# Two chunks of the next unit's first weights split earlier at the end of a pair of token slots

## The chip, the cores and the metric

One Trainium2 chip, one NeuronCore of it. The metric is device time in microseconds for one execution of the program, as the median of several runs. The core has five engines that run side by side, each its own instruction stream in program order: PE (TensorE, matrix products; PEld is its weight load), DVE (VectorE), ACT (ScalarE), POOL (GpSimd) and SP (SyncE, which only issues transfers).

## What is computed

Three layers in a row, all in 32-bit floating point: attention with random features, a feed-forward layer with softplus, and a layer of 8 experts of which each token uses one. The change lies in the last:

```python
# x: 2304 tokens x 512; E = 8 experts; w1: 8 x 512 x 1024; w2: 8 x 1024 x 512
logits = xn @ en.T / tau
expert_idx = np.argmax(logits, axis=1)
...
for e in range(E):
    mask = expert_idx == e
    h = np.maximum(x[mask] @ w1[e], 0.0)
    out[mask] = gate_w[mask, None] * (h @ w2[e])
```

## The kernel before

Tokens are sorted to experts on the chip. They are packed into slots of 128 tokens that share an expert. A unit is one slot (a single) or two slots of the same expert (a pair): first four singles, then six times a pair and a single in turn, then one more single. Two further pairs stand behind conditions at the end and run only if the routing needs them. The last 260 us of the span are these alternating units.

Each unit needs its expert's weights: `w1r` (4 chunks of 128 rows x 1024) and `w2r` (8 chunks of 128 x 512), which POOL fetches by an indirect transfer two units ahead (`fetch_w`), into one of two buffers each. PE does not multiply 32-bit numbers exactly in one pass, so every operand is split into a high and a low half: ACT casts to the high half (line 1246), DVE subtracts it from the source to get the low half (line 1250), and each product is made of three passes, high by high, high by low and low by high (`PASSES`, line 1269). The split of a chunk of first weights is `unit_w1(g, c)`, of a chunk of second weights `unit_w2(g, c)`, of the transposed token rows `unit_x(g)`. The split tiles of first weights have one buffer for each chunk and half (`wi0` to `wi7`, line 1310). So chunk c of the next unit can be split only when the present unit has used its own chunk c for the last time.

A pair works in four quarters of the hidden layer. `pair_m1(g, k)` (line 1358) makes a hidden quarter of both slots, 24 matmuls of 256 columns, six for each chunk of first weights in turn. `split(*hidden(k), ...)` takes it through relu into halves: ACT at line 1241 (`mh_h`), DVE at line 1242 (`mh_l`). `pair_m2(g, k)` (line 1382) multiplies it with two chunks of second weights into the two slots' outputs `po`, 12 matmuls of 512 columns. A single does two hidden halves: `slot_m1` (line 1335, 12 matmuls of 512 columns; for the first half in the order high and low rows by the high half of chunks 0 to 3, then high rows by the low halves, line 1275), `slot_relu` (ACT, `hs`), `slot_t` (PE transposes `pt_h`, then a split), and `slot_m2`. `unit_out` scales `po` on ACT into `ot` and has POOL scatter it to the output.

From the second unit on nothing is reordered (`tc.manual_schedule`, line 1545): each engine runs its instructions in the order in which `unit(g)` writes them (line 1395). In it `w1_(c)` splits chunk c of the next unit's first weights, `w2_(c)` of its second weights. At the end of a pair the order is: products of the last hidden quarter, three chunks of second weights, split of that hidden quarter, second products of the third quarter, the next unit's token rows, all four chunks of its first weights, second products of the last quarter, outputs, two more chunks of second weights. The next unit then starts with `slot_m1(g, 0)`.

Of the kernel before, what the change touches and what calls it, by code (L numbers as in the profile page):

```python
# [76 lines left out]
def tile_kernel(ctx, tc, q, k, v, omega, w_in, w_out, emb, tau, w1, w2, out):  # L77
# [1138 lines left out]
    def fetch_w(s, which="12", chain=0):  # L1216
        for nm, src in (("w1r", w1v), ("w2r", w2v)):
            if nm[1] not in which:
                continue
            if s < 2:  # L1220
                raw_w[nm, s] = mraw.tile([P, NC * F2], F32, name=f"{nm}{s}")
            with tc.issue_after(marks["x"]) if chain and "x" in marks and s < 4 else ExitStack():
                nc.gpsimd.indirect_dma_start(
                    out=raw_w[nm, s % 2], out_offset=None, in_=src,
                    in_offset=bass.IndirectOffsetOnAxis(ap=w_idx[:, s:s + 1].bitcast(U32), axis=0),
                    bounds_check=E * P - 1, oob_is_err=False)

    def fetch_x(g):
        t = xpool.tile([P, 2, YW], F32, tag="xhi", name="xg")
        for i, s in enumerate(groups[g]):  # L1230
            nc.gpsimd.indirect_dma_start(
                out=t[:, i, :], out_offset=None, in_=(ya if s < NS_A else yb)[:, :],
                in_offset=bass.IndirectOffsetOnAxis(ap=g_idx[:, s:s + 1].bitcast(U32), axis=0),
                bounds_check=NT - 1, oob_is_err=False)
            xgs[s] = t[:, i, :]
            if s >= NS_A:
                marks["x"] = traced()

    def split(hi, lo, lo_eng, src, relu=False, hi_eng="a"):
        if relu:  # L1240
            nc.scalar.activation(out=hi, in_=src, func=AF.Relu)
            nc.vector.scalar_tensor_tensor(out=lo, in0=src, scalar=0.0, in1=hi.bitcast(F32),
                                           op0=ALU.max, op1=ALU.subtract)
        else:
            if hi_eng == "a":
                nc.scalar.copy(out=hi, in_=src)  # L1246
            else:
                (nc.gpsimd if hi_eng == "p" else nc.vector).tensor_copy(hi, src)
            eng = nc.gpsimd if lo_eng == "p" else nc.vector
            eng.tensor_tensor(out=lo, in0=src, in1=hi.bitcast(F32), op=ALU.subtract)  # L1250
# [55 lines left out]
    def unit_w1(g, c):  # L1306
        if (g, c) in w1s:
            return
        r = raw_w["w1r", g % 2][:, c * F2:(c + 1) * F2]
        t = [wpool.tile([P, F2], F32R, tag=f"wi{2 * c + i}", name=f"w1_{c}_{i}") for i in range(2)]  # L1310
        if len(groups[g]) == 1:
            o, r = [x.rearrange("q (h p c) -> q h p c", h=2, c=4) for x in t], \
                r.rearrange("q (p h c) -> q h p c", h=2, c=4)
        else:

            o, r = [x.rearrange("q (k p j) -> q k p j", k=4, j=2) for x in t], \
                r.rearrange("q (p k j) -> q k p j", k=4, j=2)
        kind = 0 if g < 2 else len(groups[g])
        split(*o, TUNE["w1"][kind][c], r, hi_eng=TUNE["w1h"][kind][c])
        w1s[g, c] = t  # L1320

    def unit_w2(g, c):
        if (g, c) in w2s:
            return
        r = raw_w["w2r", g % 2][:, c * DM:(c + 1) * DM]
        w2s[g, c] = [wpool.tile([P, DM], F32R, tag=f"wo{2 * c + i}", name=f"w2_{c}_{i}") for i in range(2)]
        split(*w2s[g, c], TUNE["w2"][g >= 2][c], r, hi_eng=TUNE["w2h"][g >= 2][c])
# [3 lines left out]
    def hidden(key):  # L1331
        hs[key] = [ring.tile([P, 512], F32R, tag=f"wo{x}", name=f"mh_{x}") for x in "hl"]
        return hs[key]

    def slot_m1(g, half, part=slice(0, 12)):
        if part.start == 0:
            hs["ps", half] = mpsum("h", "ph")
        ph = hs["ps", half]
        w = slice(half * HF, half * HF + HF)
        mms = [(xs[g][a][c], w1s[g, c][b_][:, w]) for c, (a, b_) in first_order(half)]  # L1340
        for i in range(part.start, part.stop):
            x, r = mms[i]
            nc.tensor.matmul(ph, lhsT=x, rhs=r, start=(i == 0), stop=(i == 3 * NC - 1))  # L1343

    def slot_relu(half):
        hs["row"] = mraw.tile([P, HF], F32, tag="hs", name="hs")
        nc.scalar.activation(out=hs["row"], in_=hs["ps", half], func=AF.Relu)
# [10 lines left out]
    def pair_m1(g, k):  # L1358

        ph = hs["ps"] = mpsum("h", "ph")  # L1360
        order = first_order(k)
        for n, (c, (a, b_)) in enumerate(order):
            for j in range(2):
                f = slice(2 * k * P + j, 2 * (k + 1) * P, 2)
                nc.tensor.matmul(ph[:, j * 256:j * 256 + 256], lhsT=w1s[g, c][b_][:, f],  # L1365
                                 rhs=xs[g][a][c].rearrange("p i t -> p (i t)"),
                                 start=(n == 0 and j == 0), stop=(n == len(order) - 1), skip_group_check=True)

    def unit_m2(g, i, parts):

        s = groups[g][i]
        if parts[0][2] == 0:
            po[s] = mpsum("o", "po")
        for h, o, c in parts:
            for n, (a, b_) in enumerate(PASSES):
                nc.tensor.matmul(po[s], lhsT=h[a][:, o:o + P], rhs=w2s[g, c][b_], start=(c == 0 and n == 0),  # L1376
                                 stop=(c == 7 and n == 2))
# [4 lines left out]
    def pair_m2(g, k):  # L1382
        for i in range(2):
            unit_m2(g, i, [(hs[k], 256 * j + P * i, 2 * k + j) for j in range(2)])

    def unit_out(g):
        for s in groups[g]:
            xt = xgs.pop(s)
            ot = xpool.tile([P, DM], F32, tag="xlo", name="ot")
            nc.scalar.activation(out=ot, in_=po.pop(s), func=AF.Copy, scale=xt[:, DM:YW])  # L1390
            nc.gpsimd.indirect_dma_start(  # L1391
                out=out, out_offset=bass.IndirectOffsetOnAxis(ap=s_idx[:, s:s + 1].bitcast(U32), axis=0),
                in_=ot, in_offset=None, bounds_check=NT - 1, oob_is_err=False)

    def unit(g):
        nxt = g + 1 < NG_ALL
        ahead = g + 2 < NG_ALL

        def w1_(*cs):
            for c in cs:  # L1400
                if nxt:
                    unit_w1(g + 1, c)

        def w2_(*cs):
            for c in cs:
                if nxt:
                    unit_w2(g + 1, c)

        def fetch():
            if ahead:  # L1410
                fetch_x(g + 2)
                fetch_w(g + 2, "2", 1)

        def own(*cs):
            for c in cs:
                unit_w2(g, c)

        if ahead:
            fetch_w(g + 2, "1", 1)
        if len(groups[g]) == 2:  # L1420
            pair_m1(g, 0)
            own(2, 3, 4)
            split(*hidden(0), "v", hs["ps"], relu=True)
            pair_m1(g, 1)
            own(5)
            split(*hidden(1), "v", hs["ps"], relu=True)
            pair_m2(g, 0)
            pair_m1(g, 2)
            own(6, 7)
            fetch()  # L1430
            w2_(0)
            split(*hidden(2), "v", hs["ps"], relu=True)
            pair_m2(g, 1)
            pair_m1(g, 3)
            w2_(1, 2, 3)
            split(*hidden(3), "v", hs["ps"], relu=True)
            pair_m2(g, 2)
            if nxt:
                unit_x(g + 1)
            w1_(0, 1, 2, 3)  # L1440
            pair_m2(g, 3)
            unit_out(g)
            w2_(4, 5)
        else:
            if g > 0:
                slot_m1(g, 0)
            own(2, 3, 4)
            slot_relu(0)
            slot_m1(g, 1, slice(0, 5))
            own(5)  # L1450
            slot_t(0)
            slot_m1(g, 1, slice(5, 12))
            own(6, 7)
            slot_relu(1)
            slot_m2(g, 0, (0, 1))
            w1_(0)
            slot_t(1)
            slot_m2(g, 0, (2, 3))
            if nxt:
                unit_x(g + 1)  # L1460
            w1_(1, 2, 3)
            slot_m2(g, 1, (0, 1))
            if g == 2:
                tokens(bm_b, NT_T, NS_A, NS_B, mpsum("o", "Lb"))
            fetch()
            slot_m2(g, 1, (2, 3))
            unit_out(g)
            w2_(0, 1)
# [74 lines left out]
    for g in range(TUNE["man"]):  # L1543
        unit(g)
# [51 lines left out]
```

## Time and profile before

| what | us |
|---|---|
| median of three runs | 940.6 |
| the three runs | 940.16, 940.6, 946.91 |
| the profiled execution, its own time | 942.76 |
| its span, from the first to the last instruction | 940.9 |

The profile is of one execution. Its page gives the busy time of each engine, the views after it (waits, stretches, timelines) the single instructions with their start in us from the span's start. A timeline row merges neighbours of one kind: start, length of the whole piece, engine, line, operation, written tile and read tiles, count; brackets give the engine's idle time ahead of it and what ended that. The length of a piece of matmuls ends with the last one's modelled end, which is later than the start of the next. In the trace both kinds of weights' split tiles are called `w`; which are meant is told by the source, `w1r` or `w2r`, or by the line of the product.

### The profile page before, as it was taken

The page shows a single profiled execution, that of the slowest core. Times are in us where ns is not written, and L with a number is a line of the kernel's source. Part 1 is how long each engine was busy: PE and PEld are TensorE (multiplying, and loading weights), DVE is VectorE, ACT ScalarE, POOL GpSimd, SP SyncE. Part 2 cuts the span into 40 slices and gives each one's busy share as a digit, 9 for nine tenths or more (in the row PEclk, how much of TensorE's full clock was granted, in tenths as well). Part 3 has the DMA queues.
Part 4 walks back from the last instruction along what each step waited for, and adds up shares of the span by engine and source line. Part 5 has one row for each costly group of instructions (what it writes and reads, how often), then busy time and mean ns, then how long its engine had stood idle before and what let it go on. Part 6 is the DMA issues. An engine that isn't in the chain of part 4 may idle for free. (4 is left out here: it accounts for less than half of the span.)

```text
span 940.9 us, 14526 instructions
## 1 busy us (share of the span) xinstructions
PE 891.9 (95%) x4951; PEld 744.5 (79%) x4951; DVE 689.8 (73%) x1376; ACT 652.8 (69%) x1452; POOL 323.0 (34%) x341
## 2 busy tenths in 40 slices
PE   6898899999999999998999999999999999999993
PEld 6775555588898889987888889888797888988972
DVE  6769888477888887679886777767977676685772
ACT  4897344477878877775877687876867576585672
POOL 1224102155545754575653020012243242241310
PEclk9899999999999999999999999999999999999998
DMA  6625663011362231011301381102023660551910
GB/s 165 166 76 152 185 217 113 17 35 37 57 146 72 45 93 35 20 35 23 68 7 23 81 344 46 34 12 57 26 65 142 276 243 30 211 209 41 356 58 6
DMA packets 86540, 94.69 MB, mean 101 GB/s; under 512 B 50294, under 2 KB 74870, under 8 KB 84160
## 3 DMA queue, kind: packets, MB, share of 16 engines
q1 hardware_dynamic: 77888, 45.21, 18.5%
q0 software_dynamic: 8576, 48.52, 13.7%
q8 instruction: 41, 0.67, 0.3%
q14 instruction: 35, 0.29, 0.1%
HBM read 108.36 MB, written 15.48 MB: 132 GB/s over the span
## 5 line engine op out<-in xcount | busy, mean ns | idle before, releaser
L1376 PE MATMUL po<-w,mh_h 128*128 128x512 f32 x368 | 118.0, 402 | 0.5 <-ACT mh_h L1354 0.5
L1250 DVE TENSOR_TENSOR w<-w2r,w 128x512 fp32r<-128x512 f32 x136 | 88.4, 684 | 17.5 <-ACT w L1246 17.5
L703 PE MATMUL y<-woh,gh 128*128 128x512 f32 x240 | 96.2, 408 | 1.7 <-DVE gh L682 1.7
L1246 ACT CAST w<-w2r 128x512 fp32r<-128x512 f32 x136 | 78.7, 628 | 23.3 <-DMA w2r<-in_moe_w_dram,w_idx 12.8
L703 PE MATMUL y<-wol,gh 128*128 128x512 f32 x240 | 93.9, 395 | 0.0
L1391 POOL DMA_INDIRECT out_dram<-ot,s_idx x23 | 31.5, 1369 | 171.0 <-ACT ot L1390 126.5
L1250 DVE TENSOR_TENSOR w<-w1r,w 128x1024 fp32r<-128x1024 f32 x68 | 80.4, 1226 | 11.1 <-ACT w L1246 11.0
L703 PE MATMUL y<-woh,gl 128*128 128x512 f32 x240 | 81.7, 404 | 0.0
L598 DVE TENSOR_TENSOR wil<-win,wih 128x512 fp32r<-128x512 f32 x72 | 58.4, 811 | 29.1 <-ACT wih L597 28.9
L1376 PEld LDWEIGHTS po<-w,mh_h 128*128 128x128 f32 x368 | 66.9, 191 | 12.2 <-ACT mh_h L1354 0.7
L638 PE MATMUL h<-xhi,wih 128*128 128x384 f32 x320 | 73.0, 348 | 3.2 <-DVE t L657 2.9
L1246 ACT CAST w<-w1r 128x1024 fp32r<-128x1024 f32 x68 | 72.0, 1119 | 3.5 <-PE ph L1343 2.1
L1376 PE MATMUL po<-w,mh_l 128*128 128x512 f32 x184 | 73.4, 399 | 0.9 <-DVE mh_l L1356 0.9
L610 POOL TENSOR_TENSOR wol<-wout,woh 128x512 fp32r<-128x512 f32 x40 | 55.0, 1376 | 45.3 <-ACT woh L609 45.2
L638 PE MATMUL h<-xlo,wih 128*128 128x384 f32 x320 | 70.2, 337 | 0.0
L638 PE MATMUL h<-xhi,wil 128*128 128x384 f32 x320 | 69.9, 339 | 0.0
L1365 PE MATMUL ph<-mxh,w 128*128 128x256 f32 x384 | 62.6, 285 | 0.4
L638 PEld LDWEIGHTS h<-xhi,wih 128*128 128x128 f32 x320 | 55.4, 188 | 8.3 <-DVE t L657 3.7
L425 POOL TENSOR_TENSOR xf<-xf,rc 128x256 f32<-128x256 f32 (+1 forms) x20 | 17.3, 867 | 122.0 <-ACT rc L424 114.8
L638 PEld LDWEIGHTS h<-xhi,wil 128*128 128x128 f32 x320 | 57.7, 188 | 0.3
L1365 PEld LDWEIGHTS ph<-mxh,w 128*128 128x128 f32 x384 | 55.0, 195 | 2.9 <-ACT w L1246 1.6
L638 PEld LDWEIGHTS h<-xlo,wih 128*128 128x128 f32 x320 | 56.4, 188 | 0.0
(311 smaller groups left out, 2376.6 us busy)
## 6 DMA issues: line engine op xcount, KB each, us to landing
wst<-in_moe_w_in_dram SPq DMA_DIRECT2D x16, 512.0 KB, 4.5
wst<-in_moe_w_out_dram SPq DMA_DIRECT2D x16, 512.0 KB, 4.3
raw<-in_k_dram SPq DMA_DIRECT2D x32, 128.0 KB, 2.4
vf<-in_v_dram SPq DMA_DIRECT2D x64, 64.0 KB, 2.3
raw<-in_q_dram SPq DMA_DIRECT2D x32, 128.0 KB, 2.6
ya<-yt SPq DMA_DIRECT2D x20, 128.2 KB, 4.4
yb<-yt SPq DMA_DIRECT2D x20, 128.2 KB, 4.0
ya<-yt SPq DMA_DIRECT2D x8, 256.5 KB, 5.7
```

The source lines that it names most:

```text
L425: nc.gpsimd.tensor_tensor(out=xf, in0=xf, in1=rc, op=ALU.mult)
L598: feng("il", n).tensor_tensor(out=il, in0=wi, in1=ih.bitcast(F32), op=ALU.subtract)
L610: feng("ol", n).tensor_tensor(out=ol, in0=wo, in1=oh.bitcast(F32), op=ALU.subtract)
L638: nc.tensor.matmul(h[:, 0:G], lhsT=a[:, c, :], rhs=x[:, c, :], start=(i == 0), stop=(i == last))
L703: nc.tensor.matmul(y, lhsT=x[:, c], rhs=w, start=(f == 0 and i == 0), stop=(f == NF - 1 and i == len(passes) - 1))
L1246: nc.scalar.copy(out=hi, in_=src)
L1250: eng.tensor_tensor(out=lo, in0=src, in1=hi.bitcast(F32), op=ALU.subtract)
L1365: nc.tensor.matmul(ph[:, j * 256:j * 256 + 256], lhsT=w1s[g, c][b_][:, f], rhs=xs[g][a][c].rearrange("p i t -> p (i t)"), start=(n == 0 an ...
L1376: nc.tensor.matmul(po[s], lhsT=h[a][:, o:o + P], rhs=w2s[g, c][b_], start=(c == 0 and n == 0), stop=(c == 7 and n == 2))
L1391: nc.gpsimd.indirect_dma_start(out=out, out_offset=bass.IndirectOffsetOnAxis(ap=s_idx[:, s:s + 1].bitcast(U32), axis=0), in_=ot, in_offset ...
```

## The change

The splits of chunks 0 and 1 of the next unit's first weights are written earlier in the pair's part of `unit(g)`: chunk 0 ahead of the split of the last hidden quarter, chunk 1 behind that split and ahead of the next token rows. Chunks 2 and 3 stay where all four were. It applies to the six pairs that have a next unit.

```diff
             pair_m2(g, 1)
             pair_m1(g, 3)
             w2_(1, 2, 3)
+            w1_(0)
             split(*hidden(3), "v", hs["ps"], relu=True)
             pair_m2(g, 2)
+            w1_(1)
             if nxt:
                 unit_x(g + 1)
-            w1_(0, 1, 2, 3)
+            w1_(2, 3)
             pair_m2(g, 3)
             unit_out(g)
```

On ACT, at the end of the first pair; `w_c_0` read from `w1r` is the high half of chunk c, `mh_h` that of the last hidden quarter, `mx` that of the next token rows:

```order
 L1246 CAST w_3_0_8620<-w2r_6603 128x512
-L1241 ACTIVATE mh_h<-ph 128x512
+L1246 CAST w_0_0_8624<-w1r_6599 128x1024
+L1241 ACTIVATE mh_h<-ph 128x512
+L1246 CAST w_1_0_8644<-w1r_6599 128x1024
 L1246 CAST mx<-pt_x 128x512
-L1246 CAST w_0_0_8648<-w1r_6599 128x1024
-L1246 CAST w_1_0_8652<-w1r_6599 128x1024
 L1246 CAST w_2_0_8656<-w1r_6599 128x1024
 L1246 CAST w_3_0_8660<-w1r_6599 128x1024
```

The cast of chunk 0 has moved ahead of the relu, that of chunk 1 between the relu and the token rows; two casts are left behind the rows.

On DVE, at the same place; `w_c_1` is the low half of chunk c, `mh_l` that of the hidden quarter:

```order
 L1250 TENSOR_TENSOR w_3_1_8621<-w2r_6603,w_3_0_8620 128x512
-L1242 SCALAR_TENSOR_TENSOR mh_l<-ph,mh_h 128x512
+L1250 TENSOR_TENSOR w_0_1_8625<-w1r_6599,w_0_0_8624 128x1024
+L1242 SCALAR_TENSOR_TENSOR mh_l<-ph,mh_h 128x512
+L1250 TENSOR_TENSOR w_1_1_8645<-w1r_6599,w_1_0_8644 128x1024
 L1250 TENSOR_TENSOR mx<-pt_x,mx 128x512
-L1250 TENSOR_TENSOR w_0_1_8649<-w1r_6599,w_0_0_8648 128x1024
-L1250 TENSOR_TENSOR w_1_1_8653<-w1r_6599,w_1_0_8652 128x1024
 L1250 TENSOR_TENSOR w_2_1_8657<-w1r_6599,w_2_0_8656 128x1024
 L1250 TENSOR_TENSOR w_3_1_8661<-w1r_6599,w_3_0_8660 128x1024
```

The subtractions have moved in the same way. The order of PE, POOL and SP is the same as before.

## Rows read from the trace of the kernel before

**Rows 1.** The page, busy time of each engine over the span.

```profile
PE 891.9 (95%) x4951; PEld 744.5 (79%) x4951; DVE 689.8 (73%) x1376; ACT 652.8 (69%) x1452; POOL 323.0 (34%) x341
```

**Rows 2.** Waits from 700 us on: us in total, times, the longest.

```profile
ACT w L1246 <- DMA w2r<-in_moe_w_dram,w_idx: 12.8, 5, 3.3
...
PE ph L1343 <- DVE w L1250: 2.3, 6, 0.4
...
PE ph L1343 <- ACT w L1246: 1.3, 6, 0.2
```

**Rows 3.** Stretches, first, last of six: us; busy PE, PEld, DVE, ACT, POOL; clock, DMA.

```profile
711.69:718.96 7.27, 6.67 (x29) 4.76 (x28) 5.57 (x9) 6.02 (x11) 2.04 (x2) 1.00 0.10 36
...
899.91:907.18 7.27, 6.66 (x29) 4.76 (x28) 5.58 (x9) 6.02 (x11) 1.86 (x1) 1.00 0.11 38
```

**Rows 4.** Timeline of PE around the second boundary, from pair to single.

```profile
740.94 0.41 PE L1365 MATMUL ph<-mxl,w 128*128 128x256 f32 x2
...
743.34 0.63 PE L1376 MATMUL po<-w,mh_h 128*128 128x512 f32 x2
...
746.09 0.63 PE L1265 MATMUL pt_x<-ident,xg 128*128 128x128 f32 x4
746.48 0.72 PE L1376 MATMUL po<-w,mh_h 128*128 128x512 f32 x2
747.04 0.40 PE L1376 MATMUL po<-w,mh_l 128*128 128x512 f32 x1
...
749.34 1.65 PE L1343 MATMUL ph<-w,mx 128*128 128x512 f32 x6
751.20 1.43 PE L1343 MATMUL ph<-w,mx 128*128 128x512 f32 x5 [0.21 <-ACT w L1246]
753.02 1.65 PE L1343 MATMUL ph<-w,mx 128*128 128x512 f32 x6 [0.39 <-DVE w L1250]
754.50 0.63 PE L1265 MATMUL pt_h<-ident,hs 128*128 128x128 f32 x4
```

**Rows 5.** Timeline of PE, first products of the last single, behind a single.

```profile
913.67 4.21 PE L1343 MATMUL ph<-w,mx 128*128 128x512 f32 x17
```

**Rows 6.** Timeline of ACT around the second boundary.

```profile
743.54 0.60 ACT L1241 ACTIVATE mh_h<-ph 128x512 fp32r<-128x512 f32 x1 [2.25 <-PE ph L1365]
746.76 0.59 ACT L1246 CAST mx<-pt_x 128x512 fp32r<-128x512 f32 x1 [2.62 <-PE pt_x L1265]
747.25 3.90 ACT L1246 CAST w<-w1r 128x1024 fp32r<-128x1024 f32 x4
751.05 1.26 ACT L1390 ACTIVATE ot<-po,xg 128x512 f32<-128x512 f32 x2
752.20 1.13 ACT L1246 CAST w<-w2r 128x512 fp32r<-128x512 f32 x2
753.55 0.60 ACT L1347 ACTIVATE hs<-ph 128x512 f32<-128x512 f32 x1 [0.22 <-PE ph L1343]
```

**Rows 7.** Timeline of DVE around the second boundary.

```profile
744.17 0.69 DVE L1242 SCALAR_TENSOR_TENSOR mh_l<-ph,mh_h 128x512 fp32r<-128x512 f32 x1 [2.16 <-ACT mh_h L1241]
747.38 0.69 DVE L1250 TENSOR_TENSOR mx<-pt_x,mx 128x512 fp32r<-128x512 f32 x1 [2.52 <-ACT mx L1246]
748.33 4.63 DVE L1250 TENSOR_TENSOR w<-w1r,w 128x1024 fp32r<-128x1024 f32 x4 [0.25 <-ACT w L1246]
```

**Rows 8.** Timeline of POOL: the fetch of first weights used at the second boundary.

```profile
720.08 1.04 POOL L1223 DMA_INDIRECT w1r<-in_moe_w_dram,w_idx  x1 [0.30 <-issue]
```

**Rows 9.** All of w1r: duration ns min/median/max, first and last start; transfer to landing.

```profile
L1246 ACT CAST w<-w1r x68: 1031/1052/1344, 552.7 to 913.5; 128x1024 fp32r<-128x1024 f32 x68
L1250 DVE TENSOR_TENSOR w<-w1r,w x68: 1201/1222/1278, 559.4 to 914.9; 128x1024 fp32r<-128x1024 f32 x68
...
DMA to landing us min/median/max: 2.1/8.3/11.5
```

## The prediction

> **What bounds the kernel now.** I read the page's first part, then the table of waits of the last third, then the stretches around the place of the change, then the timelines of PE, ACT and DVE there. PE is busy for 95% of the span and no other engine passes 79% [rows 1], so time can only be won where PE stands still or starts late. In the table of waits, 700 us to the end, PE's first products (line 1343) wait six times for ACT's `w` and six times for DVE's `w` [rows 2]. Six is the number of pairs that run, each followed by a single slot. The stretch from such a single's first product to its first second product takes 7.27 us at the first and at the last of the six boundaries, at a granted clock of 1.00 (the 2.4 GHz level), with PE busy 6.67 us [rows 3]. So the stall is the same at each, and one boundary can stand for all.
>
> At the second boundary PE reads: last quarter of the pair from 746.48, the single's first products at 749.34, a restart at 751.20 behind ACT, another at 753.02 behind DVE, the transposes of the hidden row at 754.50 [rows 4]. The busy share hides part of the loss, since a matmul's modelled end outlasts the next start; I count from start to start. The pace without such waits is shown by the last single, which follows a single: 17 products of the same shape in 4.21 us [rows 5]; less one length of 0.40 (a 512-column matmul in [rows 4]), 3.81 over 16 steps, or 0.238 us each.
>
> **What the stall is made of.** ACT is idle for 2.25 us ahead of the relu at 743.54, that is from 741.29, and for 2.62 from 744.14 to 746.76; then it casts the token rows and all four weight chunks in one go, 747.25 to 751.15 [rows 6]. DVE runs behind it: idle for 2.16 up to 744.17, that is from 742.01, and for 2.52 up to 747.38, then four subtractions up to 752.96 [rows 7]. The single needs the high half of chunk 3 for its 7th product and its low half for the 12th. Undisturbed the 7th starts at 749.34 + 6 x 0.238 = 750.77, but it starts at 751.20, behind the last cast: 0.43 us. From there the 12th is due at 752.39 and starts at 753.02, behind the last subtraction: 0.63. Over all, 17 x 0.238 = 4.05 puts the transposes at 753.39; they stand at 754.50, so 1.11 us are lost, the rest of it in small waits.
>
> **The change, part by part.** No instruction is added or removed; at each pair two casts and two subtractions move, and no DMA is issued by them. A w1r cast takes 1.05 us and a subtraction 1.22 (medians, [rows 9]).
>
> Chunk 0 goes ahead of the split of the last hidden quarter (`hidden(3)`). Its cast has two new conditions: the weights must have landed, and the pair's own last reader of that tile must be through. That reader is the 6th matmul of the last hidden quarter, 740.94 + 0.41 = 741.35 [rows 4]; the cast can run 741.4 to 742.45. ACT next wants the relu of `ph` at 743.54, so it loses nothing with 1.1 us to spare. The subtraction runs 742.5 to 743.7; DVE next starts `mh_l` at 744.17, 0.4 us later [rows 7]. Behind these two stand, on ACT the relu, on DVE `mh_l`, and for both of them PE's last quarter; that needs `mh_h` at 746.48 and `mh_l` at 747.04 [rows 4], 2.3 and 2.2 us after they are ready. So even if the 0.4 us were gone the cost is nothing until 2.2 us more are used up. Chunk 1 follows at 744.04 to 745.1 on ACT (it starts where the relu lets go, as in [rows 6]) and 745.1 to 746.3 on DVE, in the idle time ahead of the token rows at 746.76 and 747.38, whose time PE's transposes set. Nothing is delayed.
>
> What stays behind the rows is chunks 2 and 3: casts 747.25 to 748.3 and 748.2 to 749.3, subtractions 748.35 to 749.55 and 749.5 to 750.7. The 7th product (750.77) then has 1.5 us to spare, and the 12th (749.34 + 11 x 0.238 = 751.96) 1.25. Both waits go.
>
> What is late next: the transposes at 753.39 need the relu'd row `hs`. The 12th product ends at 751.96 + 0.40 = 752.36, `hs` takes 0.60 [rows 6] and is ready at 753.0: 0.4 us in hand. ACT must be free by then: the two outputs (the second cannot start before the pair's last product ends, about 749.5) and two w2 casts end near 751.3. So the whole 1.11 comes back, and everything after it shifts with PE.
>
> The queue that is moved: POOL scatters the outputs and issues the next loads behind them. The first output starts at 751.05 now and about 749.2 then, so that queue comes up to 1.8 us earlier while PE comes 1.1 earlier. The next second weights, for which ACT waits 12.8 us in five places [rows 2], thus land no later relative to PE. SP issues nothing in this part.
>
> The sum: 6 x 1.11 = 6.7 us. The moved instructions cost 0 by the idle rows; no row shows a cast of w1r beside the last hidden quarter's products, so its duration there is bounded by the quickest and the slowest of 68, 1.03 and 1.34 against a median of 1.05 [rows 9]; neither 0.02 less nor 0.3 more matters within 1.1 us of room. I take 0. The profiled execution took 942.76 us (span 940.9), which makes 936.1; the median of the three runs is 2.2 us lower, so I forecast 933.9.
>
> **A rule against the pace.** The rows give 0.238 us per product without waits [rows 5]. The Trainium skill, TensorE: Matmul & The Clock Gate, section Back-to-back issue gap, states N / 2.4 + 2.5 ns for a single 512-column matmul at full clock, 216 ns; by it 17 products would take 3.67 us, the loss would be 1.49 per boundary, and the gain an estimated 8.9 us. The rows do not bear it out: the last single and the pair's last quarter (12 products from 746.48 to 749.34) both run at 0.238, the quickest stretch, the quarter before, 12 products from 743.34 to 746.09, at 0.229 [rows 4, 5]. So the sum goes by 0.238.
>
> **The rivals.**
> *A, the wait moves on.* The `hs` row or the outputs ahead of it come no earlier, and the transposes stay where they are. For it: only 0.4 us of room at `hs`. Against it: ACT is free a full 1 us ahead. If all 1.11 comes back as a wait, the time is 940.6.
> *B, one wait of the two goes.* DVE has the least room (0.4 us ahead of `mh_l`), and if its tail stayed as long, the 0.63 at the 12th product would remain: gain 6 x 0.43 = 2.6, 938.0.
> *C, slower.* Chunk 0's cast now stands ahead of the relu on ACT. If it cannot start at 741.4, the relu and `mh_l` wait behind it. A start at s lets `mh_l` end at s + 1.05 + 1.22 + 0.69, about s + 2.95; it is needed at 747.04, so it costs from s = 744.1 and outweighs the 1.11 from s = 745.2. If it started only at its old place among the casts, 747.25, the last quarter would be 3.15 us late: 6 x (3.15 - 1.11) = 12.2 us more, 952.8. For it: a wait for a transfer is put ahead of something PE needs. Against it: the first weights were issued at 720.08 [rows 8] and the slowest of them took 11.5 us [rows 9], so 731.6 at the latest, ten us ahead; and even if the cast waited for the whole hidden quarter it would start near 743.6. The Trainium skill (TensorE: Matmul & The Clock Gate, section Architectural detail) says that ACT and DVE are strict FIFO; by that nothing would overtake the held cast, as this rival has it, and the rows show each engine in program order.
> *D, a quicker pace.* If the freed products ran at the pace of the quickest stretch, 0.229, 17 of them would take 3.89, the loss be 1.27 a boundary and the gain 7.6: 933.0. (By the estimate from the page it would be 931.7.) For it: that stretch is of the same shape. Against it: the last single, the same line and operands, does not reach it.
>
> **How the numbers follow.** Forecast 0.75, A 0.06, B 0.07, C 0.04, D 0.08. Runs of this kernel that agree lie within 0.5 us of each other (940.16, 940.6), one lies 6 above; a measurement can tell about 1%, 9.4 us, from no change. The forecast with its unknowns spans 932.5 to 936; D and the scatter of runs take the low end to 931, B and that scatter the high end to 939; A and C stay out. Over 1% faster would need more than D and the scatter together: half of D's chance, 0.04. Over 1% slower is C, 0.04. The rest, 0.92, lies within 1%.
>
> **What would show it.** Right: in the changed profile a w1r cast stands ahead of the last relu of each pair, starting 0.1 us after the 6th product of the last hidden quarter; relu and last quarter keep their distance; the single's 17 products run with no restart, and the stretch from its first product to its first second product is near 6.15 us instead of 7.27, six times. The two rows "PE ph waits for w" are gone. Wrong: a longer time from the last hidden quarter to the last quarter's products (C), a new wait at the transposes for `hs` (A), a restart behind DVE that stays (B), or a stretch that is right while the total is not, which would mean that the 6.7 us are given back elsewhere, the second weights' landing first.

## The result, and the profile after

The changed kernel takes 933.47 us, median of five runs (932.06 to 935.02), against 940.6 for before (five runs, 940.16 to 946.91). The ratio is 0.9911 with a 95% interval of 0.9891 to 0.993: 0.9% faster, 6.6 to 10.3 us. The forecast was 933.9, in a range of 931 to 939, and a gain within 1%. The profiled execution took 933.47 with a span of 931.7.

The page of the changed kernel, busy time of each engine, answers to [rows 1]:

```profile
span 931.7 us, 14532 instructions
...
PE 888.7 (95%) x4951; PEld 746.3 (80%) x4951; DVE 691.7 (74%) x1376; ACT 653.7 (70%) x1452; POOL 320.9 (34%) x341
```

The shares have hardly moved: the work is the same, and some eight microseconds of waiting in 940 do not show in a share. The stretches show it. From the single's first product to its first second product, the changed kernel's first, second and last boundary, columns as in [rows 3]:

```profile
710.91:716.86 5.95, 5.95 (x30) 4.99 (x28) 3.39 (x7) 4.13 (x9) 2.49 (x2) 1.00 0.12 44
747.27:753.23 5.96, 5.96 (x30) 4.99 (x29) 3.40 (x7) 4.14 (x9) 2.48 (x2) 1.00 0.12 44
892.74:898.69 5.95, 5.95 (x29) 4.99 (x28) 3.39 (x7) 4.13 (x9) 1.48 (x1) 1.00 0.14 47
```

7.27 us have become 5.95, PE is busy through all of it, and DVE and ACT each do two pieces of work less here (9 and 11 instructions before, 7 and 9 now): no subtraction or cast of first weights is left in it. All six boundaries show 5.95 or 5.96.

The timeline of PE at the second boundary, answering to [rows 4]:

```profile
738.88 0.41 PE L1365 MATMUL ph<-mxl,w 128*128 128x256 f32 x2
...
744.03 0.63 PE L1265 MATMUL pt_x<-ident,xg 128*128 128x128 f32 x4
744.42 0.72 PE L1376 MATMUL po<-w,mh_h 128*128 128x512 f32 x2
744.97 0.40 PE L1376 MATMUL po<-w,mh_l 128*128 128x512 f32 x1
...
747.27 4.02 PE L1343 MATMUL ph<-w,mx 128*128 128x512 f32 x17
751.13 0.63 PE L1265 MATMUL pt_h<-ident,hs 128*128 128x128 f32 x4
```

The three pieces of the first products with their two restarts are one row of 17. From start to start it lasts 751.13 - 747.27 = 3.86 us, 5.16 before. Ahead of it nothing has stretched: 3.24 from the token rows' transposes to the single (744.03 to 747.27), 3.25 before.

ACT and DVE of the changed kernel at the same place, answering to [rows 6] and [rows 7]:

```profile
739.32 1.05 ACT L1246 CAST w<-w1r 128x1024 fp32r<-128x1024 f32 x1
741.48 0.60 ACT L1241 ACTIVATE mh_h<-ph 128x512 fp32r<-128x512 f32 x1 [1.11 <-PE ph L1365]
741.98 1.05 ACT L1246 CAST w<-w1r 128x1024 fp32r<-128x1024 f32 x1
744.70 0.59 ACT L1246 CAST mx<-pt_x 128x512 fp32r<-128x512 f32 x1 [1.68 <-PE pt_x L1265]
745.18 2.01 ACT L1246 CAST w<-w1r 128x1024 fp32r<-128x1024 f32 x2
747.09 1.27 ACT L1390 ACTIVATE ot<-po,xg 128x512 f32<-128x512 f32 x2
...
750.19 0.60 ACT L1347 ACTIVATE hs<-ph 128x512 f32<-128x512 f32 x1 [0.81 <-PE ph L1343]
```

```profile
740.41 1.22 DVE L1250 TENSOR_TENSOR w<-w1r,w 128x1024 fp32r<-128x1024 f32 x1 [0.45 <-ACT w L1246]
742.11 0.69 DVE L1242 SCALAR_TENSOR_TENSOR mh_l<-ph,mh_h 128x512 fp32r<-128x512 f32 x1 [0.48 <-ACT mh_h L1241]
743.05 1.23 DVE L1250 TENSOR_TENSOR w<-w1r,w 128x1024 fp32r<-128x1024 f32 x1 [0.25 <-ACT w L1246]
745.32 0.69 DVE L1250 TENSOR_TENSOR mx<-pt_x,mx 128x512 fp32r<-128x512 f32 x1 [1.04 <-ACT mx L1246]
746.27 2.36 DVE L1250 TENSOR_TENSOR w<-w1r,w 128x1024 fp32r<-128x1024 f32 x2 [0.26 <-ACT w L1246]
```

Chunk 0's cast starts 0.03 us behind the end of the 6th product of the last hidden quarter (738.88 + 0.41 = 739.29). The brackets give the room that is left: 1.11 us ahead of the relu, 0.48 ahead of `mh_l`. The outputs start 0.18 us ahead of the single's first product, 1.71 behind it before.

Where the 9.2 us between the two spans lie: between the first boundary's single and the last single's first product there are 201.98 us before (711.69 to 913.67) and 194.26 after (710.91 to 905.17), so 7.7 in the changed part. The other 0.8 ahead of it and 0.7 behind it lie in code that is the same in both kernels. Over six profiles of the changed kernel and of versions that leave the end as it is, the last single's first product stands 26.3 to 27.1 us ahead of the end, and 27.3 in that of before. Ahead of the changed part the scatter is larger: in these profiles the first boundary's single starts at 710.2 to 713.0 us (for the version with four chunks ahead, below, its own 0.8 taken off), in that of before at 711.69. Differences of this size thus stand between runs of the same code; of before there is one profile.

### The profile page after: what moved, and what is told of

Read it like the earlier page. It is cut to its first block, busy times and chain, and to the rows that moved or that the text cites. A ratio compares the mean times of both kernels' runs of the same rounds, so it can differ in the third digit from the quotient of the medians.

```text
span 931.7 us, 14532 instructions
## 1 busy us (share of the span) xinstructions
PE 888.7 (95%) x4951; PEld 746.3 (80%) x4951; DVE 691.7 (74%) x1376; ACT 653.7 (70%) x1452; POOL 320.9 (34%) x341
## 5 line engine op out<-in xcount | busy, mean ns | idle before, releaser
L1391 POOL DMA_INDIRECT out_dram<-ot,s_idx x23 | 29.3, 1275 | 166.7 <-ACT ot L1390 122.1
L653 ACT ACTIVATE r<-h 128x384 f32<-128x384 f32 x64 | 31.6, 494 | 36.0 <-PE h L638 35.6
```

The costliest lines, as they stand in the source:

```text
L653: nc.scalar.activation(out=r, in_=h[:, 0:G], func=AF.Relu)
L1391: nc.gpsimd.indirect_dma_start(out=out, out_offset=bass.IndirectOffsetOnAxis(ap=s_idx[:, s:s + 1].bitcast(U32), axis=0), in_=ot, in_offset ...
```

## The experiments

The theory: the gain is the two waits at six boundaries and nothing else (T). Its rivals: the earlier outputs and the loads behind them on POOL bring part of it (R), and the cast ahead of the relu costs something that the gain covers (C). All edits are to the changed kernel; each ratio is to the kernel before, run beside it.

**One chunk only, ahead of the relu.**

```diff
             split(*hidden(3), "v", hs["ps"], relu=True)
             pair_m2(g, 2)
-            w1_(1)
             if nxt:
                 unit_x(g + 1)
-            w1_(2, 3)
+            w1_(1, 2, 3)
```

> Chunk 0 alone stays ahead of the last hidden split; chunks 1, 2 and 3 stand behind the token rows. Theory T (the gain is the two waits at the six boundaries, and nothing else): with three casts behind the rows the last cast ends about 0.5 us ahead of the 7th product, the last subtraction ends within 0.1 us of the 12th. So the restart behind ACT is gone, the one behind DVE is 0 to 0.15, and the 17 products take 3.86 to 4.05 us from start to start (5.16 before, 3.86 with the change). 0 to 1 us slower than the changed kernel in all. Rival R (part of the gain comes from the outputs and loads that POOL issues earlier): outputs stand 1 us later on ACT than in the changed kernel, so the time would lie between before and the change, about 4 us above the change.

Measured: 935.47 us, ratio 0.9925 (0.9903 to 0.9946). The stretch of 17 products is 4.05 to 4.07 us at all six boundaries, so one moved chunk brings 1.11 of the 1.30 and the second the last 0.19. Six times 0.19 is 1.1 us, just above the 0 to 1 that were expected; the ratios stand 0.0014 apart, 1.3 us, with intervals that overlap. R would have it about 4 us above the change. The timeline of PE in this kernel at the second boundary, and the waits of its weight loads, in us in total, times, longest:

```profile
747.27 4.21 PE L1343 MATMUL ph<-w,mx 128*128 128x512 f32 x17
751.33 0.63 PE L1265 MATMUL pt_h<-ident,hs 128*128 128x128 f32 x4
```

```profile
PEld ph L1343 <- DVE w L1250: 2.2, 7, 0.3
```

The row of 17 products has no bracket and no break, and yet it is 0.19 longer than in the changed kernel (4.21, 4.02). PE's own row hides the wait, because the modelled end of the product before it covers it; only PEld shows it, 0.3 us at seven places. Six are the boundaries, the seventh is the last single, whose row of 4.21 us is [rows 5]. The expectation put the loss at the 12th product at 0 to 0.15; it is 0.19.

**One chunk only, behind the relu.**

```diff
-            w1_(0)
             split(*hidden(3), "v", hs["ps"], relu=True)
             pair_m2(g, 2)
-            w1_(1)
+            w1_(0)
             if nxt:
                 unit_x(g + 1)
-            w1_(2, 3)
+            w1_(1, 2, 3)
```

> One chunk moved as well, but behind the last hidden split, not ahead of it; three chunks behind the rows. Theory T: same as the run with chunk 0 ahead, within 0.5 us, since the place ahead of the relu costs nothing. Rival C (the cast ahead of the relu holds the last quarter up): this one would be quicker than the run with chunk 0 ahead, by 0.1 us or more a boundary, and the distance from the last hidden quarter's first product to the last quarter's first product would be shorter here.

Measured: 935.44 us, ratio 0.9927 (0.9905 to 0.995), the stretch of 17 products 4.05 at all six, and 3.24 or 3.25 us from the token rows' transposes to the single's first product, as in the run above and in both kernels. The distance that the expectation names, from the last hidden quarter's first product to the last quarter's first, is 6.01 us at every boundary of all four. So a cast ahead of the relu costs nothing that can be seen: C falls for one chunk.

**All four chunks ahead of the relu.**

```diff
-            w1_(0)
+            w1_(0, 1, 2, 3)
             split(*hidden(3), "v", hs["ps"], relu=True)
             pair_m2(g, 2)
-            w1_(1)
             if nxt:
                 unit_x(g + 1)
-            w1_(2, 3)
```

> All four chunks ahead of the last hidden split. Theory T with the strict order of each engine: four casts from 741.4 to 745.3 in the times of the kernel before, the relu 745.2 to 745.8, the last subtraction ends near 747.15, mh_l 747.8 where the last quarter's third product wants it at 747.04: PE waits for mh_l about 0.8 us at each of six boundaries, 17 products run free in 3.86, so 4.9 us slower than the changed kernel and about 3 us faster than before. If the room ahead of the relu were larger than I count: no wait for mh_l and the same time as the changed kernel. If it were smaller: over 1.3 us a boundary, slower than before.

Measured: 939.62 us, ratio 0.9963 (0.9944 to 0.9981). ACT, DVE and PE of this kernel at the second boundary:

```profile
742.17 3.92 ACT L1246 CAST w<-w1r 128x1024 fp32r<-128x1024 f32 x4
746.00 0.58 ACT L1241 ACTIVATE mh_h<-ph 128x512 fp32r<-128x512 f32 x1
```

```profile
743.25 4.63 DVE L1250 TENSOR_TENSOR w<-w1r,w 128x1024 fp32r<-128x1024 f32 x4 [0.45 <-ACT w L1246]
747.80 0.68 DVE L1242 SCALAR_TENSOR_TENSOR mh_l<-ph,mh_h 128x512 fp32r<-128x512 f32 x1
```

```profile
743.89 0.40 PE L1365 MATMUL ph<-mxl,w 128*128 128x256 f32 x2
...
746.88 0.63 PE L1265 MATMUL pt_x<-ident,xg 128*128 128x128 f32 x4
747.27 0.72 PE L1376 MATMUL po<-w,mh_h 128*128 128x512 f32 x2
748.54 0.50 PE L1376 MATMUL po<-w,mh_l 128*128 128x512 f32 x1 [0.56 <-DVE mh_l L1242]
...
750.93 4.02 PE L1343 MATMUL ph<-w,mx 128*128 128x512 f32 x17
```

The hidden quarter is ready for its relu at 744.29 (743.89 + 0.40), but the relu comes when the fourth cast is done and `mh_l` when the fourth subtraction is; the last quarter's third product starts 748.54 - 747.27 = 1.27 us behind its first, 0.55 in the changed kernel. The transposes stand 4.05 to 4.07 ahead of the single, 3.24 in the changed kernel: 0.81 us at each boundary, where 0.8 was expected. The 17 products run free. Against the changed kernel's 0.9911 the ratio is 0.0052 higher, 4.9 us of 943 (the median of before beside this run is 942.97), as expected. So the hold that rival C supposes is real, and four chunks cost what was expected of them; with one chunk it has not begun. The Trainium skill (TensorE: Matmul & The Clock Gate, Architectural detail) calls ACT and DVE strict FIFO; here the relu starts at 746.00, as the casts end, and the trace agrees.

**Outputs behind the next second weights.**

```diff
             pair_m2(g, 3)
+            w2_(4, 5)
             unit_out(g)
-            w2_(4, 5)
```

> The changed kernel, with the pair's outputs behind the two second-weight chunks on ACT instead of ahead of them; the outputs' casts and so POOL's scatter and the loads behind it start 0.9 to 1.2 us later. Theory T: nothing on PE moves, same time as the changed kernel within 0.5 us, ACT's waits for second weights in transfer grow by about 1 us each from 7.9 in five but stay ahead of the relu. Rival R: the loads decide part of the gain, 1 us later a boundary costs up to 6 us.

Measured: 934.04 us, ratio 0.9913 (0.9884 to 0.9943), against 0.9911 of the changed kernel. All six stretches are 5.95 us. What did move is ACT's wait for second weights in transfer, in this kernel and then in the changed kernel:

```profile
ACT w L1246 <- DMA w2r<-in_moe_w_dram,w_idx: 12.7, 5, 3.1
```

```profile
ACT w L1246 <- DMA w2r<-in_moe_w_dram,w_idx: 7.9, 5, 1.9
```

4.8 us more of waiting on ACT in five places cost no time: behind that wait stands the relu of the third quarter, and it still waits for something else at each of the five, 0.31 us at the least, behind the longest wait for weights. By this edit the loads behind the outputs are issued 0.6 to 1.2 us later against the single's first product, of the 1.9 to 2.5 by which the change had brought them earlier, so alone it tests only a part of R. The rest of a cycle settles it: from one boundary's first second product to the next boundary's first product lie 30.37 us before ((899.91 - 711.69) / 5 - 7.27) and 30.42 with the change ((892.74 - 710.91) / 5 - 5.95), so the earlier loads bring nothing there. R falls. Nor is the sum of these waits steady: 12.8 before [rows 2], 7.9 in this profile of the change and 10.1 in its second, below.

**The changed kernel again, and a version that goes on.** The same was done in the singles from the fifth unit on: their next unit's chunk 1 goes ahead of the next token rows.

```diff
             slot_m2(g, 0, (2, 3))
+            if g >= NS_A:
+                w1_(1)
             if nxt:
                 unit_x(g + 1)
             w1_(1, 2, 3)
```

A chunk that has been split is not split again, so the later call does chunks 2 and 3.

> The changed kernel once more, beside the next one on the same chip. Theory T: six stretches of 5.95 us from the single's first product to its first second product, as in its first profile; 7.7 us less than before within the alternating units (six times 1.28, the distance of the first boundary to the last single's first product), and what the span differs beyond that is scatter of the parts that the change doesn't touch, so a ratio of 0.990 to 0.993.

> The change, and in each single behind the first four chunk 1 of the next unit's first weights ahead of the next token rows as well. In the profiles so far the pair's first products lose 0.5 us behind ACT's last cast at each single to pair boundary (five of them), and the last single's first 17 products and transposes take 4.59 us against 3.86 undisturbed. Theory T: the pair's products run free (0.24 from the third to the fourth chunk, now 0.75), the last single comes to 3.9 to 4.0: 5 x 0.5 + 0.6 = 3.1 us less than the changed kernel, ratio to before near 0.988. If the idle time on ACT ahead of the rows (1.2 us for a cast of 1.05) does not hold it, or DVE's rows come late for the pair's third product, the gain is 0 to 1 us or turns to a loss.

Measured, on one chip: the change 934.25 us, ratio 0.9909 (0.9882 to 0.9935), six stretches of 5.95 or 5.96; the version that goes on 930.12, ratio 0.9867 (0.9844 to 0.9891), 4.1 us less by the medians, and the quickest of all kernels run here. A pair's first products behind a single, of the changed kernel's second profile and then of the version that goes on:

```profile
725.21 0.40 PE L1365 MATMUL ph<-mxh,w 128*128 128x256 f32 x2
725.45 0.40 PE L1365 MATMUL ph<-mxl,w 128*128 128x256 f32 x2
725.91 0.51 PE L1365 MATMUL ph<-mxh,w 128*128 128x256 f32 x2
```

```profile
724.45 0.40 PE L1365 MATMUL ph<-mxh,w 128*128 128x256 f32 x2
724.69 0.40 PE L1365 MATMUL ph<-mxl,w 128*128 128x256 f32 x2
724.93 0.40 PE L1365 MATMUL ph<-mxh,w 128*128 128x256 f32 x2
725.17 0.40 PE L1365 MATMUL ph<-mxl,w 128*128 128x256 f32 x2
```

The step from the third chunk's last products to the fourth chunk (725.45 to 725.91) takes 0.46 us (0.51 in the first profile); it has become the 0.24 of the others. That is 0.22 to 0.27 at this boundary, not the 0.5 that I had expected from a wrong difference: I took 0.75, which is two steps, against the 0.24 of one. Yet the distance from boundary to boundary fell by 0.4 to 0.5 us, to 35.89 (782.37 - 746.48) from 36.29 (783.99 - 747.70). The pair's first two hidden quarters, from its first product to its first second product, hold it: 730.43 - 724.26 = 6.17 with the change, 729.25 - 723.50 = 5.75 here. Of these 0.42, 0.22 is the step to the fourth chunk, 0.11 the step behind it (0.35 and 0.24) and 0.10 lies in the next twelve products:

```profile
726.50 1.70 PE L1365 MATMUL ph<-mxh,w 128*128 128x256 f32 x12
```

```profile
725.41 1.60 PE L1365 MATMUL ph<-mxh,w 128*128 128x256 f32 x12
```

Again a stretch that is longer without a bracket. The low half that it waits for is that of chunk 3. DVE's three subtractions in the changed kernel's second profile:

```profile
723.59 3.56 DVE L1250 TENSOR_TENSOR w<-w1r,w 128x1024 fp32r<-128x1024 f32 x3 [0.27 <-ACT w L1246]
```

They end at 727.15, and the 23rd of the quarter's 24 products, the first with chunk 3's low half, has its weights loaded from 727.21; the step behind it is 0.22 us in place of 0.12. The last single's 17 products take 4.02 us in place of 4.21, and its transposes come 4.03 us behind the first of them in place of 4.59. In the traces the version gains 2.2 us from the first boundary's single to the last single's first product (194.08 and 191.86) and 0.56 behind it, 2.8 in all where 3.1 was expected; the medians say 4.1, with the scatter of the untouched parts in them.

```profile
902.46 4.02 PE L1343 MATMUL ph<-w,mx 128*128 128x512 f32 x17
906.49 0.75 PE L1265 MATMUL pt_h<-ident,hs 128*128 128x128 f32 x4
```

## Why the prediction was right, point by point

**The place and the mechanism held.** The two waits were the ones named, six times, equal at each; both are gone, and no row "PE ph waits for w" is left from 690 us on. The moved work lies where it was said to lie: the cast 0.03 us behind the product that frees the tile (0.1 forecast), 1.11 and 0.48 us of room (1.1 and 0.4), `hs` ready 0.34 us ahead of the transposes (750.19 + 0.60 against 751.13; 0.4 forecast). On PE nothing ahead of the single's first product moved.

**One term was mis-sized: the loss per boundary, "1.11 us are lost".** It is 5.16 - 3.86 = 1.30, and the stretch forecast near 6.15 us came out at 5.95. The step that failed is "the pace without such waits is shown by the last single". That row is not without waits. It has the same late low half of chunk 3 behind DVE, 0.19 us, which no bracket on PE shows. The change leaves that row as it is, and in the changed kernel, from 700 us on, one such wait of the weight loads is left, at this row's 12th product:

```profile
PEld ph L1343 <- DVE w L1250: 0.3, 1, 0.3
```

The run with one chunk moved makes a row of the same length, 4.21, out of exactly that wait, and the version that goes on brings the last single itself to 4.02. The pace free of waits is 3.86 / 17 = 0.227 us, 3.81 over 16 in the forecast being 0.238. The second witness for 0.238, the pair's last quarter, runs at 0.230 from its third product on ((749.34 - 747.04) / 10 in [rows 4]); what makes it 0.238 is its head, right behind the transposes, where two products take 0.56 us, as they do with the change (744.42 to 744.97). So the quickest stretch of [rows 4], 0.229, was the right row, and rival D's arithmetic, 6 x 1.27 = 7.6, comes nearest: measured in the changed part are 7.7 (7.9 in the change's second profile, 201.98 - 194.08). The forecast of 6.7 stood 1.0 short.

The estimate that the Trainium skill allows (TensorE: Matmul & The Clock Gate, Back-to-back issue gap), 216 ns for a single product and by it 8.9 us, is not reached: 227 ns is what the trace shows with nothing to wait for and a granted clock of 1.00.

**Of 6 x 1.32 = 7.9 us saved in the stretches 7.7 arrive.** The rest lies at the next wait, the pair's first products behind a single: 0.47 us from third to fourth chunk before (727.11 to 727.58 on PE), 0.51 with the change (725.00 to 725.51). ACT's three casts there stand behind token rows that wait for PE's transposes, so they have moved with PE: they start 1.98 us ahead of the pair's first product in both (723.93 to 725.91 before, 721.83 to 723.81 with the change) and took 3.63 us in place of 3.59. That is no fixed price: in the change's second profile the step is 0.43 to 0.47.

**The rivals.** A, the wait moving to `hs`: no, the transposes wait for nothing. B, the wait behind DVE staying: no; even with one chunk moved only 0.19 us of it is left, and 85% of the gain is there. C did not arise, since chunk 0's cast started 0.03 us behind the product that frees its tile; that work ahead of the relu can hold it is shown by the run with four chunks: one chunk 0 us, four chunks 0.81 us a boundary. D, the pace: right in size, for the reason that its evidence was the row without a wait.

**The total.** The ratio's interval, 6.6 to 10.3 us, holds the forecast gain of 6.7 at its edge and the 7.7 well inside. That the median came within 0.4 us of the forecast is in part luck: the sum was 1.0 short in the changed part, and the median of before that it starts from, 940.6, is the lowest of the three measured (942.97 of 22 runs and 942.23 of 11 beside the experiments). The 9.2 between the profiled spans is not the gain: 1.5 of it lie outside the changed part.

## What to carry to other kernels

In queues that run in order, look for idle time ahead of an instruction that waits for another engine, and put there work that stands in a burst behind it; here its price was 0 while it ended before the wait did, and work that ran past it was paid for (0 for one chunk, 0.81 us a boundary for four). Before a row is taken as the undisturbed pace, look at the weight loads' waits for it and at a second stretch of the same shape: a wait shorter than a matmul's modelled end leaves no gap on PE's row. And when the first burst is taken apart, look for the same burst at the next boundary: here it was worth another 2.8 us in the traces.

## What I had not expected

Little has to move: two of the four casts and subtractions taken out of the burst bring 1.30 us, one alone brings 1.11 of it. The version that goes on gained 0.42 us in a pair's first two quarters where the step that I had seen was 0.22: the other half lay in the products behind it, without a gap on PE's row. And the wait for second weights in transfer varies from 7.9 to 10.1 us between two profiles of the same kernel, while the six stretches stay at 5.95.
